# One attention and feed-forward kernel on one core: token chunks taken from one batch, and the second weight matrix kept on the chip for the first unit

## The chip, the core and the metric

The kernel runs on one core of a Trainium2 chip. A core has TensorE (matrix products; its weight loads are a row of their own, PEld, in the profile), VectorE (DVE), ScalarE (ACT), GpSimd (POOL) and SyncE (SP), which here issues most of the DMA transfers. TensorE writes its results to PSUM, from which VectorE and ScalarE read them. Each engine works through its own instructions in the order in which the program issued them, and waits where an operand is not ready. The metric is the time of one execution on the device in microseconds (us); lower is better. The time before is 1080.71 us, the median of three runs.

## What is computed

An attention block without softmax, normed per head, feeds a feed-forward block with a squared ReLU:

```
q, k, v: (8, 8, 576, 64)   # batch, head, position, width of a head; fp32
kv  = einsum('bhsd,bhse->bhde', k, v)          # one 64x64 matrix per batch and head
o   = einsum('bhsd,bhde->bhse', q, kv)
x   = o / sqrt(mean(o*o, -1) + 1e-6) * g_norm  # then (batch*position, head*width) = (4608, 512)
h   = x @ w_in                                 # w_in (512, 2048)
g   = s * max(h, 0)**2 + b
out = g @ w_out                                # w_out (2048, 512)
```

Both weight matrices come to the kernel in a 64-bit type, so that each has to be brought to fp32 on the chip.

## The kernel before

**Tokens.** There are 36 chunks of 128 tokens, numbered c, and 9 units u of four chunks. A chunk takes 64 tokens from each of two batches (a pair is called a group g; positions p*9 + j for one j), so the first chunk needs the k and v of two batches. `load_kv` (L89) brings half of the heads of a group, `load_q` (L102) the q of two chunks.

**kv and attention.** `kv_product` (L271) forms the 64x64 matrices in 64-row, 64-column matmuls and copies them (L292) into `bd_kv`, block diagonal by pairs of heads, with one such block set for each of the two batches. `attention` (L296) has three steps for each chunk: `turn` transposes q (L305, copied at L307), `product` multiplies by `bd_kv` (L317) in two half products per pair of heads, one for each batch, then squares (L326, ACT), sums (L328, DVE), takes the root (L330, ACT) and its reciprocal (L332) and scales (L334, DVE); `turn_x` transposes the result (L342) and copies it to `xT` (L345). `x_sums` (L351) forms four further operands.

**The two large products.** Each is done by a 2x2 block scheme with seven products in place of eight (named x1, z2, x6, y7, x5, x3, y4), whose operands are sums and differences of the blocks and whose results are built up in PSUM banks x, y and z. `mm1` (L386) runs it for each of four strips s of w_in: `keep` (L394) copies a partial result r1, r2 or r4 out of bank x before the next product adds to that bank, VectorE adds it to bank z or y (L164), and `relu_sq` (L383) squares the positive part. The results `ga` stay on the chip. `mm2` (L454) does the same with w_out, for two halves j of a unit; `s2` and `s4` are four VectorE instructions each, on `ga`. It reads the operands of w_out from a ring of three buffers, filled by `load_w2` (L446, issued at L448), one 1 MB transfer per product. The attention of the next unit and `x_sums` run between the steps of mm2 (`side_of`, L607). In every unit x3 and y4 of the last strip come after the first step of mm2.

**The weights.** `load_w` (L119) brings one of sixteen blocks (eight of w_in, eight of w_out, L128 and L133) into one of three raw buffers. `round_w` (L139) converts it: two instructions on ScalarE (L155, L156), then two on VectorE (L158 after L155, L161 after L156). `sum_w_in` (L177) makes further operands of a strip of w_in. `make_w_out` (L203) converts two blocks of w_out, forms the operands for mm2, and stores all seven operand sets to DRAM in pieces (L216 to L223), and `finish_w_out` (L227) adds the blocks to `bias_row` (L259), the row sums times b on TensorE, and makes and stores the last set. All of w_out thus goes to DRAM and comes back for every unit.

**The order.** It is written out by hand. First come the loads and `kv_product` of group 0, the attention of chunks 0 to 3 and the conversion of the first blocks; then mm1 of unit 0, with conversions put between its steps by a table (`in_first`, L641); then the rest of w_out, the loads of q, of the next group's k and v and of the first two w_out operands (all on SP); then mm2 of unit 0. The later units repeat mm1 and mm2; the kv products of groups 1, 2 and 3 are spread over the steps of mm1 in three of them.

Of the kernel before, what the change touches and what calls it, by code (L numbers as in the profile page):

```python
# [15 lines left out]
def kernel(  # L16
# [32 lines left out]

    nc = tc.nc  # L50
# [20 lines left out]
    xp = ctx.enter_context(tc.tile_pool(name="xp", bufs=2))  # L71
    rp = ctx.enter_context(tc.tile_pool(name="rp", bufs=2))
# [14 lines left out]
    HH = H // 2  # L87

    def load_kv(g, half, pool, queues=(nc.sync, nc.sync)):  # L89

        for name, src, queue in zip("kv", (k, v), queues):
            t = pool.tile([P, HH, R, D], FP32, name=f"{name}_sb", tag=name)
            for s in range(2):
                queue.dma_start(
                    out=t[s * HB : s * HB + HB].rearrange("p h j d -> p h (j d)"),
                    in_=src[2 * g + s, half * HH : half * HH + HH].rearrange(
                        "h (p j) d -> p h (j d)", j=R
                    ),
                )
            kv_in[name, g, half] = t  # L100

    def load_q(c, queue=nc.sync):  # L102

        t = qp.tile([P, 2, H, D], FP32, name="q_sb", tag="q")
        for i in range(2):
            g, j = divmod(c + i, R)
            for s in range(2):
                queue.dma_start(  # L108
                    out=t[s * HB : s * HB + HB, i],
                    in_=q[2 * g + s].rearrange("h (p j) d -> p j h d", j=R)[:, j],  # L110
                )
            q_in[c + i] = t[:, i]
# [6 lines left out]
    def load_w(i):  # L119

        dst = convp.tile([P, 2 * words * DM], U32 if wide else FP32, name="w_raw", tag="raw", bufs=3)
# [77 lines left out]
    W2_AT = {1: 0, 7: 1, 5: 2, 6: 3, 4: 4, 2: 5, 3: 6}  # L199
    w2_dram = dram.tile([P, 7, FC // 2, HN], FP32, name="w2")  # L200
    w_up, w_dn = {}, {}

    def make_w_out(s):  # L203

        up = w_up[s] = convp.tile([P, 2, DM], FP32, name="w_up", tag="up", bufs=2)
        dn = w_dn[s] = convp.tile([P, 2, DM], FP32, name="w_dn", tag="dn", bufs=2)
        t = convp.tile([P, 3, 2, HN], FP32, name="w_t", tag="wt", bufs=2)
        b11, b12 = up[:, :, :HN], up[:, :, HN:]
        b21, b22 = dn[:, :, :HN], dn[:, :, HN:]
        t1, t2, t4 = (t[:, i] for i in range(3))  # L210
        blocks = slice(2 * s, 2 * s + 2)

        round_w(FC + 2 * s, up.rearrange("p b n -> p (b n)"))
        sub(t1, b12, b11)
        send_w()
        nc.sync.dma_start(out=w2_dram[:, 0, blocks], in_=b11)  # L216
        round_w(FC + FC // 2 + 2 * s, dn.rearrange("p b n -> p (b n)"))
        sub(t2, b22, t1)
        sub(t4, b21, t2)
        send_w()  # L220
        nc.sync.dma_start(out=w2_dram[:, 2:5, blocks], in_=t)
        for half in range(2):
            nc.sync.dma_start(  # L223
                out=w2_dram[:, 5 + half, blocks], in_=dn[:, :, half * HN : half * HN + HN]
            )

    def finish_w_out(s):  # L227

        bias_row(w_up[s], s == 0, False)
        bias_row(w_dn[s], False, s == NS - 1)  # L230
        b12, b22 = w_up[s][:, :, HN:], w_dn[s][:, :, HN:]
        sub(b12, b22, b12)
        nc.sync.dma_start(out=w2_dram[:, 1, 2 * s : 2 * s + 2], in_=b12)
# [6 lines left out]
    bd_kv = [const.tile([P, 2, NP, P], FP32, name=f"bd_kv_{i}") for i in range(2)]  # L240
# [18 lines left out]
    def bias_row(w, first, last):  # L259

        if first:
            b_ps.append(ps_t.tile([P, DM], FP32, name="b_ps", tag="t"))
        for b in range(2):
            matmul(b_ps[0], b_sq, w[:, b], first and b == 0, last and b == 1)
        if last:
            nc.scalar.copy(b_row, b_ps[0])


    kv_ps = {}

    def kv_product(g, p):  # L271

        if p == 0:
            kv_ps[g] = [ps_t.tile([P, NP, D], FP32, name="kv_ps", tag="t") for _ in range(2)]
        half, h0 = divmod(2 * p, HH)
        kt, vt = kv_in["k", g, half], kv_in["v", g, half]
        for j in range(R):
            for l in range(2):
                for s in range(2):
                    rows = slice(s * HB, s * HB + HB)  # L280
                    nc.tensor.matmul(  # L281
                        kv_ps[g][s][l * HB : l * HB + HB, p, :],
                        lhsT=kt[rows, h0 + l, j, :],
                        rhs=vt[rows, h0 + l, j, :],
                        start=(j == 0),
                        stop=(j == R - 1),
                    )
        if p == NP - 1:
            for s in range(2):
                for l in range(2):  # L290
                    ls = slice(l * HB, l * HB + HB)
                    nc.scalar.copy(bd_kv[g % 2][ls, s, :, ls], kv_ps[g][s][ls])  # L292
# [3 lines left out]
    def attention(c, first=False):  # L296


        bd = bd_kv[c // R % 2]
# [9 lines left out]
        def product():  # L309
# [4 lines left out]
            for p in range(NP):  # L314
                for s in range(2):
                    half = slice(s * HB, s * HB + HB)
                    nc.tensor.matmul(  # L317
                        ps[half, p, :],
                        lhsT=st["qT"][:, p, half],
                        rhs=bd[:, s, p, :],  # L320
                        start=True,
                        stop=True,
                    )
            x = ps.rearrange("p c (l d) -> p (c l) d", l=2)
            sq = attp.tile([P, H, D], FP32, name="sq", tag="sq", bufs=1)
            nc.scalar.activation(sq, x, AF.Square)  # L326
            ss = attp.tile([P, H], FP32, name="ss", tag="ss")
            nc.vector.reduce_sum(ss, sq, axis=mybir.AxisListType.X)  # L328
# [4 lines left out]
            st["xn"] = attp.tile([P, H, D], FP32, name="xn", tag="xn")  # L333
# [4 lines left out]
        def turn_x():  # L338
# [4 lines left out]
            if j == 0:  # L343
                xT[u] = xp.tile([P, KC, 2 * TB], FP32, name="xT", tag="xT", bufs=1)
# [6 lines left out]
    def x_sums(u):  # L351
        b11, b12 = xT[u][:, :KH, :TB], xT[u][:, :KH, TB:]
        b21, b22 = xT[u][:, KH:, :TB], xT[u][:, KH:, TB:]
        for i in (5, 7, 6, 4):
            xs[u, i] = xp.tile([P, KH, TB], FP32, name=f"xs_{i}", tag=f"xs_{i}", bufs=1)
# [27 lines left out]
    def relu_sq(t):  # L383
        nc.vector.scalar_tensor_tensor(t, t, 0.0, t, ALU.max, ALU.mult)  # L384

    def mm1(u, s):  # L386
# [7 lines left out]
        def keep(name, src):  # L394
            st[name] = rp.tile([P, 2, TB], FP32, name=name, tag=name)
            nc.scalar.copy(st[name], src)  # L396

        def x1():
            st["x"] = bank_of("x", "x")
            mm1_product(1, u, s, st["x"], True)  # L400
            keep("r1", st["x"])

        def z2():
# [4 lines left out]
            relu_sq(t)  # L408

        def x6():  # L410
            mm1_product(6, u, s, st["x"], False)
            keep("r2", st["x"])
# [5 lines left out]
        def x5():  # L418
            mm1_product(5, u, s, st["x"], False)
            keep("r4", st["x"])  # L420
            t = g_tile("a22")
            add(t, st["y"], st["r4"])
            relu_sq(t)

        def x3():
# [4 lines left out]
            add(g_tile("s1"), t, ga["a22", s])  # L430
            sub(t, ga["a11", s], t)

        def y4():
# [3 lines left out]
            relu_sq(t)  # L437
# [8 lines left out]
    def load_w2(u, n):  # L446
        t = late["ring"].tile([P, FC // 2, HN], FP32, name="w2_sb", tag="w2")
        nc.sync.dma_start(out=t, in_=w2_dram[:, W2_AT[ORDER[n]]])  # L448
        ring[u, ORDER[n]] = t

    out_v = out.rearrange("(bp j) n -> bp j n", j=R)
    G_OF = {1: "a11", 2: "a12", 3: "a12", 4: "a22", 5: "s1", 6: "a11", 7: "a21"}

    def mm2(u):  # L454
        st = {}

        def product(i, j, ps, first):
            for f in range(FC // 2):
                s, b = divmod(f, 2)
                matmul(  # L460
                    ps, ga[G_OF[i], s][:, b, j * P : j * P + P], ring[u, i][:, f, :],
# [255 lines left out]
```

## Time and profile before

| | |
|---|---|
| Runs | 1077.69, 1080.71, 1099.49 us |
| The profiled execution | 1076.64 us, its span (first to last instruction) 1074.8 us |
| TensorE busy | 999.6 us, 93% of the span |
| VectorE busy | 451.2 us, 42% |
| ScalarE busy | 202.8 us, 19% |
| Moved by DMA | 128.84 MB, 120 GB/s over the span |

The page cuts the span into 40 slices of 26.9 us and gives the busy share of each engine in tenths (9 is 90% or more), and the clock that TensorE was granted, in tenths:

```profile
PE   1788609999999999999999999999999999999998
DVE  0398704244423442444235424443354244524441
ACT  0544400211121112111211121112111211121100
PEclk9889859999999999999999999999999999999999
```

In a timeline row stand the start in us, the length in us, the engine, the line, the operation, what it writes and reads with shapes, and the number of instructions merged; in brackets, how long the engine was idle before and what ended that. In a grouped row the time after the bar is the busy time of the group in us and the mean of one instruction in ns, then the idle time before. A row of transfers has the number, the size of one and the median us from issue to landing.

### The profile page before, as it was taken

To read this page: it belongs to the slowest core of one execution; us is meant where nothing else is said; L and a number is where in the kernel's file an instruction comes from. 1 tells how busy PE (TensorE), PEld (TensorE's weight loads), DVE (VectorE), ACT (ScalarE), POOL (GpSimd) and SP (SyncE) were. 2 spreads that over 40 slices of the span, in tenths; PEclk is the share of its full clock that TensorE was granted. 3 is DMA by queue.
4 is the path that set the end of the run, shared out by engine and by line. 5 is a ranking of instruction groups with operands and counts; after the bars stand their busy time and mean duration, and the time that the engine had idled before them with its cause. 6 is when DMAs were issued, how large, how long until landed. Compare 5 with 4: busy or idle time off the path is not lost.

```text
span 1074.8 us, 13966 instructions
## 1 busy us (share of the span) xinstructions
PE 999.6 (93%) x6080; PEld 857.4 (80%) x6080; DVE 451.2 (42%) x733; ACT 202.8 (19%) x338; POOL 2.5 (0%) x8
## 2 busy tenths in 40 slices
PE   1788609999999999999999999999999999999998
PEld 1577208888888888888888888888888888888887
DVE  0398704244423442444235424443354244524441
ACT  0544400211121112111211121112111211121100
POOL 0000000000000000000000000000000000000000
PEclk9889859999999999999999999999999999999999
DMA  9556792245227222452273224522602260224032
GB/s 196 176 196 215 285 269 101 88 148 128 79 79 210 75 79 88 148 128 79 79 206 79 79 88 147 129 79 79 196 1 79 82 194 1 79 88 147 1 118 79
DMA packets 73838, 128.84 MB, mean 120 GB/s; under 512 B 41136, under 2 KB 45232, under 8 KB 65712
## 3 DMA queue, kind: packets, MB, share of 16 engines
q1 hardware_dynamic: 70128, 125.06, 37.9%
q10 hardware_dynamic: 3648, 2.89, 1.3%
q8 instruction: 48, 0.79, 0.3%
q14 instruction: 14, 0.11, 0.0%
HBM read 111.15 MB, written 16.78 MB: 119 GB/s over the span
## 4 chain that ended last, share of the span: by engine, by line
PE 86%; DMA 5%; DVE 5%; ACT 2%; SPq 1%; issue 1%; ACTq 0%; DVEq 0%
PE x_ps L82 45%; PE y_ps L82 25%; PE z_ps L82 8%; PE x_ps L317 3%; PE kv_ps L281 2%; DMA v_sb<-in_v_dram 2%; PE qT_ps L305 1%; PE xT_ps L342 1%; DMA w_sb<-w 1%; DMA w_raw<-in_moe_w_out_dram 1%; DMA s_col<-in_moe_s_dram 1%; ACT w_raw L156 1%; DMA w_raw<-in_moe_w_in_dram 1%; SPq L108 0%; ACT w_raw L155 0%
## 5 line engine op out<-in xcount | busy, mean ns | idle before, releaser
L82 PE MATMUL x_ps<-w_sb,a 128*128 128x256 f32 x864 | 197.5, 384 | 24.2 <-DMA w_sb<-w 24.2
L82 PEld LDWEIGHTS x_ps<-w_sb,a 128*128 128x128 f32 x864 | 163.6, 192 | 50.1 <-issue 28.5
L82 PE MATMUL y_ps<-w_sb,a 128*128 128x256 f32 x720 | 162.0, 380 | 0.0
L82 PEld LDWEIGHTS y_ps<-w_sb,a 128*128 128x128 f32 x720 | 134.3, 190 | 18.3 <-issue 1.4
L82 PE MATMUL x_ps<-xs,ws 128*128 128x256 f32 x576 | 138.2, 383 | 6.0 <-DVE ws L167 6.0
L82 PE MATMUL y_ps<-xs,wb 128*128 128x256 f32 x576 | 137.7, 382 | 3.4 <-DVE a L164 3.4
L396 ACT COPY r<-x_ps 128x512 f32<-128x512 f32 x108 | 63.3, 586 | 350.9 <-PE x_ps L82 350.9
L82 PEld LDWEIGHTS x_ps<-xs,ws 128*128 128x128 f32 x576 | 110.2, 192 | 21.7 <-issue 6.4
L82 PEld LDWEIGHTS y_ps<-xs,wb 128*128 128x128 f32 x576 | 110.1, 192 | 19.1 <-DVE a L164 3.8
L164 DVE TENSOR_TENSOR a<-y_ps,r 128x512 f32<-128x512 f32 x72 | 49.5, 688 | 138.0 <-ACT r L396 138.0
L466 DVE SCALAR_TENSOR_TENSOR or<-x_ps,s_col,b_row 128x256 f32<-128x256 f32 x54 | 26.1, 483 | 125.2 <-PE x_ps L82 125.2
L384 DVE SCALAR_TENSOR_TENSOR a<-a 128x512 f32<-128x512 f32 x108 | 74.7, 692 | 3.7
L82 PE MATMUL x_ps<-xT,wa 128*128 128x256 f32 x288 | 70.2, 388 | 1.7 <-DVE wa L161 1.7
L82 PE MATMUL x_ps<-xT,ws 128*128 128x256 f32 x288 | 68.5, 380 | 0.2 <-ACT r L396 0.2
L82 PE MATMUL z_ps<-xT,wa 128*128 128x256 f32 x288 | 68.3, 380 | 0.0
L328 DVE TENSOR_REDUCE ss<-sq 128x8 f32<-128x512 f32 x36 | 24.7, 685 | 103.4 <-ACT sq L326 103.3
L82 PE MATMUL x_ps<-w_sb,s 128*128 128x256 f32 x288 | 65.8, 382 | 0.0
L82 PEld LDWEIGHTS x_ps<-xT,wa 128*128 128x128 f32 x288 | 55.5, 194 | 9.9 <-DVE wa L161 2.1
L82 PEld LDWEIGHTS z_ps<-xT,wa 128*128 128x128 f32 x288 | 55.0, 191 | 7.6
L82 PEld LDWEIGHTS x_ps<-xT,ws 128*128 128x128 f32 x288 | 54.4, 190 | 8.0 <-ACT r L396 0.6
L82 PEld LDWEIGHTS x_ps<-w_sb,s 128*128 128x128 f32 x288 | 53.4, 190 | 8.0 <-issue 1.4
L429 DVE TENSOR_TENSOR a<-a 128x512 f32<-128x512 f32 x36 | 24.9, 692 | 73.9 <-ACT a L428 73.9
(64 smaller groups left out, 692.0 us busy)
## 6 DMA issues: line engine op xcount, KB each, us to landing
w_sb<-w SPq DMA_DIRECT2D x63, 1024.0 KB, 5.0
k_sb<-in_k_dram SPq DMA_DIRECT2D x16, 576.0 KB, 7.6
out_dram<-o SPq DMA_DIRECT2D x36, 256.0 KB, 2.1
q_sb<-in_q_dram SPq DMA_DIRECT2D x68, 128.0 KB, 4.5
w_raw<-in_moe_w_in_dram SPq DMA_DIRECT2D x8, 1024.0 KB, 6.4
w_raw<-in_moe_w_out_dram SPq DMA_DIRECT2D x8, 1024.0 KB, 5.8
v_sb<-in_v_dram SPq DMA_DIRECT2D x12, 576.0 KB, 11.5
w<-w_t SPq DMA_DIRECT2D x4, 768.0 KB, 6.8
```

Of the source, the lines that this page charges most:

```text
L82: nc.tensor.matmul(o, lhsT=lhsT, rhs=rhs, start=start, stop=stop, skip_group_check=True)
L156: nc.scalar.activation(lo, lo, AF.Copy, scale=2.0**-29)
L164: nc.vector.tensor_tensor(out=o, in0=a, in1=b, op=ALU.add)
L281: nc.tensor.matmul(kv_ps[g][s][l * HB : l * HB + HB, p, :], lhsT=kt[rows, h0 + l, j, :], rhs=vt[rows, h0 + l, j, :], start=(j == 0), stop= ...
L305: nc.tensor.transpose(ps[:, p, :], q_in[c][:, 2 * p : 2 * p + 2, :], ident)
L317: nc.tensor.matmul(ps[half, p, :], lhsT=st["qT"][:, p, half], rhs=bd[:, s, p, :], start=True, stop=True,)
L328: nc.vector.reduce_sum(ss, sq, axis=mybir.AxisListType.X)
L342: nc.tensor.transpose(ps[:, p, :], st["xn"][:, 2 * p : 2 * p + 2, :], ident)
L384: nc.vector.scalar_tensor_tensor(t, t, 0.0, t, ALU.max, ALU.mult)
L396: nc.scalar.copy(st[name], src)
L429: nc.vector.tensor_mul(t, t, t)
L466: nc.vector.scalar_tensor_tensor(o, ps, s_col, other, ALU.mult, ALU.add)
```

## The change

A chunk is now 128 tokens of one batch: positions j = i and j = 4 + i for i = 0 to 3, and a fifth chunk per pair of batches that takes j = 8 of both (`halves`). k, v, the kv products and `bd_kv` go by batch: `kv_product` runs for one batch in one piece, batch 0 in the head, batch 1 after the third step of mm2 of unit 0, batches 2 to 7 after slot 12 of mm1 of units 1 to 6. `product` does one full matmul per pair of heads where the chunk has one batch. Output rows leave in two transfers per chunk.

For unit 0, w_out's blocks stay on the chip in `w_up` and `w_dn`. Every one of the fourteen conversions after the first two stands at a slot of mm1 (one after it), `bias_row` follows, and the operand sets are formed in place during mm2, each after the product that used the old contents and after the store of them; every set is stored once for the later units. Unit 0 has no ring loads. In unit 0 the squares of z2 and y4 move to ScalarE, the sums s1 and a21 of `ga` are put off to the end of mm1 (`g_sums`), and x3 and y4 of the last strip come before mm2. Several pools go to one buffer, r1 and r4 share one, and the square of the attention output shares a buffer with the scaled output. The first two ring loads of a unit are issued at the end of the unit before.

```diff
+    def halves(c):
+        g, i = divmod(c, R)
+        if i == 4:
+            return [(2 * g, R - 1), (2 * g + 1, R - 1)]
+        b, i = (2 * g, i) if i < 4 else (2 * g + 1, i - 5)
+        return [(b, i), (b, 4 + i)]
...
+    w_up = convp.tile([P, FC // 2, DM], FP32, name="w_up")
+    w_dn = convp.tile([P, FC // 2, DM], FP32, name="w_dn")
+    W2_AT = {
+        1: w_up[:, :, :HN], 6: w_up[:, :, :HN], 5: w_up[:, :, :HN], 7: w_up[:, :, HN:],
+        2: w_dn[:, :, :HN], 4: w_dn[:, :, :HN], 3: w_dn[:, :, HN:],
+    }
+    def sum_w_out(i, fn, a, b):
+        for s in range(NS):
+            blocks = slice(2 * s, 2 * s + 2)
+            fn(W2_AT[i][:, blocks], W2_AT[a][:, blocks], W2_AT[b][:, blocks])
+    def store_w2(*which):
+        for i in which:
+            nc.sync.dma_start(out=w2_dram[i], in_=W2_AT[i])
...
             for p in range(NP):
+                if b == b1:
+                    matmul(ps[:, p, :], st["qT"][:, p, :], bd_kv[b % 2][:, p, :], True, True)
+                    continue
                 for s in range(2):
...
-    def relu_sq(t):
-        nc.vector.scalar_tensor_tensor(t, t, 0.0, t, ALU.max, ALU.mult)
+    def relu_sq(t, on_act):
+        if on_act:
+            nc.scalar.activation(t, t, AF.Relu)
+            nc.scalar.activation(t, t, AF.Square)
+        else:
+            nc.vector.scalar_tensor_tensor(t, t, 0.0, t, ALU.max, ALU.mult)
+    def g_sums(s):
+        add(ga["s1", s], ga["a21", s], ga["a22", s])
+        sub(ga["a21", s], ga["a11", s], ga["a21", s])
...
+        def t2():
+            if u == 0:
+                sum_w_out(6, add, 7, 1)
+                store_w2(6)
+        def t4():
+            if u == 0:
+                sum_w_out(4, sub, 2, 6)
+                store_w2(4)
+        def t1():
+            if u == 0:
+                sum_w_out(5, sub, 3, 6)
+                store_w2(5)
         return [
             lambda: x1(0),
-            seq(lambda: x1(1), nxt(2), s2),
+            seq(lambda: x1(1), nxt(2), t2, s2),
             lambda: z2(0),
-            seq(lambda: z2(1), nxt(3), s4),
+            seq(lambda: z2(1), nxt(3), s4, t4),
             lambda: x6(0),
-            seq(lambda: x6(1), nxt(4)),
+            seq(lambda: x6(1), nxt(4), t1),
...
+    def convert(n):
+        s, lower = divmod(n % FC, 2)
+        if n < FC // 2:
+            round_w_in(s, lower)
+            send_w()
+            if lower:
+                sum_w_in(s)
+        else:
+            round_w_out(s - NS, lower)
+            send_w()
...
-    in_first = {0: (convert_w_in, 1), 4: (convert_w_in, 2), 11: (convert_w_in, 3), 17: (make_w_out, 0)}
+    at_slot = {0: 2, 2: 3, 4: 4, 7: 5, 9: 6, 12: 7, 15: 8, 18: 9, 20: 10, 22: 11, 24: 12, 26: 13, 27: 14}
...
         if u == 0:
-            finish_w_out(0)
-            for s in range(1, NS):
-                make_w_out(s)
-                finish_w_out(s)
-            tc_late()
+            convert(15)
+            for i in range(2):
+                load_kv(1, i, convp, tag="raw", bufs=3)
             loads(0)
-            load_w2(0, 0)
-            load_w2(0, 1)
+            bias_row()
+            store_w2(1, 2, 3)
+            sum_w_out(7, sub, 3, 7)
+            store_w2(7)
+            for s in range(NS):
+                g_sums(s)
```

More of the change, by code (lines that the diff above doesn't have):

```diff
@@ L257 @@
     b_ps = []
[L259 to L277, printed above, removed]
-            for l in range(2):
[L279 to L292, printed above, removed]
@@ new lines, in bias_row, with kv_product @@
+    def bias_row():
+        ps = ps_t.tile([P, DM], FP32, name="b_ps", tag="t")
+        blocks = [w[:, 2 * s + b] for s in range(NS) for w in (w_up, w_dn) for b in range(2)]
+        for n, w in enumerate(blocks):
+            matmul(ps, b_sq, w, n == 0, n == FC - 1)
+        nc.scalar.copy(b_row, ps)
+    def kv_product(b):
+        ps = [ps_t.tile([P, 2, D], FP32, name="kv_ps", tag="t") for _ in range(2)]
+        for i in range(2):
+            kv = kv_in.pop((b, i))
+            for j in range(R):
+                for l in range(2):
+                    for r in range(2):
+                        rows = slice(r * HB, r * HB + HB)
+                        nc.tensor.matmul(
+                            ps[r][l * HB : l * HB + HB, i, :],
+                            lhsT=kv[rows, 0, l, j, :],
+                            rhs=kv[rows, 1, l, j, :],
+                            start=(j == 0),
+                            stop=(j == R - 1),
+                        )
+        for r in range(2):
+            for l in range(2):
+                ls = slice(l * HB, l * HB + HB)
+                nc.scalar.copy(bd_kv[b % 2][ls, 2 * r : 2 * r + 2, ls], ps[r][ls])
@@ L580 @@
         send_w()
-    for p in range(NP):
-        kv_product(0, p)
+    kv_product(0)
     kv0p.release()
```

191 lines of the change are left out of this document (85 added, 106 removed).

## The prediction

> **What bounds the kernel now.** I read the busy time by stage first, then the timeline of the head and of the first unit, then one late unit on TensorE, and the chain of waits at the one long hole. In the stage rows the columns are window, length, busy PE, PEld, DVE, ACT, POOL, granted clock, DMA share, GB/s.
>
> ```profile
> span 1074.8 us, 13966 instructions
> 0.00:46.70 46.70, 18.11 (x384) 15.07 (x384) 8.73 (x17) 12.50 (x23) 2.48 (x8) 0.90 0.80 192
> 46.70:106.80 60.10, 50.50 (x208) 42.72 (x209) 50.37 (x70) 26.37 (x32) 0.00 (x0) 0.91 0.59 201
> 106.80:159.20 52.40, 19.35 (x34) 6.68 (x32) 21.18 (x27) 14.05 (x14) 0.00 (x0) 0.68 0.88 268
> 171.88:1029.43 857.55, 857.55 (x5217) 745.93 (x5217) 355.96 (x592) 149.27 (x268) 0.00 (x0) 1.00 0.34 101
> 819.26:924.35 105.09, 105.09 (x546) 91.67 (x545) 44.50 (x74) 18.11 (x32) 0.00 (x0) 1.00 0.28 91
> 603.47:714.18 110.71, 110.71 (x833) 95.89 (x833) 44.48 (x74) 19.57 (x36) 0.00 (x0) 1.00 0.37 108
> 145.01 13.77 DMA w_sb<-w
> 159.23 5.74 PE L82 MATMUL x_ps<-w_sb,a 128*128 128x256 f32 x16 [24.23 <-DMA w_sb<-w]
> ```
>
> From 171.88 us, where z2 of the first unit's mm2 starts, TensorE has no gap, at full clock: a unit takes 105.09 us, 110.71 with a pair of batches' kv products, so a wait there must become a gap before it costs, and only fewer TensorE cycles gain. Before it, 172 us hold one unit's worth of TensorE work: the head waits for k and v, the first mm1 runs beside VectorE (50 of 60 us busy), and from 106.8 to 159.2 TensorE does 19 us of work while w_out is converted, sent to DRAM and read back. That is what the change touches.
>
> **The head.** Before, two batches' k and v land; afterwards one batch's.
>
> ```profile
> 16.22 4.03 PE L281 MATMUL kv_ps<-v_sb,k_sb 64*64 64x64 f32 x142 [3.27 <-DMA v_sb<-in_v_dram]
> 27.18 3.71 PE L281 MATMUL kv_ps<-v_sb,k_sb 64*64 64x64 f32 x142 [5.11 <-DMA v_sb<-in_v_dram]
> 30.97 1.51 ACT L292 COPY bd_kv<-kv_ps 64x256 f32<-64x256 f32 x4 [28.96 <-PE kv_ps L281]
> 45.30 0.67 ACT L345 ACTIVATE xT<-xT_ps,g_col 128x512 f32<-128x512 f32 x1
> 46.70 3.78 PE L82 MATMUL x_ps<-xT,wa 128*128 128x256 f32 x8 [1.67 <-DVE wa L161]
> ```
>
> The first half-load, whose bytes equal one batch's, was complete at 16.2. I keep 16.2: transfers are half as large, but q moves up beside them. Then the second pair of heads' products, half of 3.71 (1.9), and four copies of half the width, 0.26 each by estimate from 0.38: 19.2 against 32.5. From there to the fourth xT (45.97) are 13.5 us of unchanged attention. Call that end E: 45.97 before, 32.7 afterwards. w_raw follows q with 10 us to spare.
>
> **The first mm1.** Afterwards it carries all sixteen conversions, on in-order queues.
>
> ```profile
> L155 ACT ACTIVATE w_raw<-w_raw 128x1024 f32<-128x1024 f32 x16 | 18.6, 1160 | 9.2 <-DMA w_raw<-in_moe_w_out_dram 9.2
> L156 ACT ACTIVATE w_raw<-w_raw 128x1024 uint32<-128x1024 uint32 x16 | 18.5, 1157 | 0.0
> L158 DVE TENSOR_SCALAR w_dn<-w_raw 128x1024 uint32<-128x1024 uint32 x4 | 2.8, 689 | 0.4 <-ACT w_raw L155 0.4
> L161 DVE CUSTOM_DVE_ANT_0 w_dn<-w_raw,w_dn 128x2048 uint16<-128x2048 uint16 x4 | 4.9, 1225 | 0.8 <-ACT w_raw L156 0.3
> L167 DVE TENSOR_TENSOR ws<-ws,wa 128x512 f32<-128x512 f32 x4 | 2.8, 692 | 0.1
> L164 DVE TENSOR_TENSOR a<-y_ps,r 128x512 f32<-128x512 f32 x72 | 49.5, 688 | 138.0 <-ACT r L396 138.0
> L396 ACT COPY r<-x_ps 128x512 f32<-128x512 f32 x108 | 63.3, 586 | 350.9 <-PE x_ps L82 350.9
> L428 ACT ACTIVATE a<-x_ps 128x512 f32<-128x512 f32 x36 | 21.5, 598 | 100.1 <-PE x_ps L82 100.1
> 106.99 1.88 PE L82 MATMUL b_ps<-w_up,b_sq 128*128 128x512 f32 x4
> 108.71 1.88 PE L82 MATMUL b_ps<-w_dn,b_sq 128*128 128x512 f32 x4
> w_raw<-in_moe_w_out_dram SPq DMA_DIRECT2D x8, 1024.0 KB, 5.8
> w<-w_t SPq DMA_DIRECT2D x4, 768.0 KB, 6.8
> ```
>
> A conversion is 2.2 us on ACT (two instructions overlapping a little), then 1.25 on DVE for its last step; sum_w_in 2.6 (four overlapping L167 of 0.69); an add 0.7; Relu then Square, now on ACT for z2 and y4 of unit 0, 1.2; a keep copy 0.6; a warm mm1 product 1.73, a cold one up to 3.8 (the 46.70 row). The move to ACT makes a ring: the Square waits for DVE's add, the add stands behind a conversion on DVE, that waits for ACT, and the next keep, which lets TensorE write the x bank again, stands behind all of it. I follow the start of x5 in each strip, in us after E. Strip 0: conv0's last step and cold x1 to 4.55, keep 0.6, conv1 2.1 on ACT, 1.2 on DVE, two sums 1.5, so x6 at 10.0; conv2's end and z2's add on DVE to 13.75, 1.2, keep to 15.5, y7 ending at 16.4: x5 at 16.4. Strip 1: conv3 behind that keep (2.1, 1.25) and its sum_w_in 2.6 end at 21.4; then x5's add and relu 1.4, conv4 2.0, x3's multiply and z2's add 1.3, ACT 1.2, conv5 2.2 and 1.2, sums 2.6, y4's add 0.6, ACT 1.2, keep 0.6: 35.7. Strip 2: cold x5 3.8, x1 2.9, keep 0.6, conv7 2.1 and 1.3, sums 2.6, three DVE steps 1.9, ACT 2.4 less 0.7 that overlaps, conv8 2.1, keep 0.5: 55.2. Strip 3 the same way without sums, conv9 to conv11: 16.3, so 71.5. To the end: x5 2.3, keep 0.6, x3 1.9, Relu 0.6, conv13 2.2 and 1.2, add 0.7, ACT 1.2, conv14 and conv15 4.3, last DVE step 1.3: 87.8. Each block's load goes out at least 9 us before its turn, against 5.8 to land.
>
> Bias_row, 32 instructions of 0.43 (four in 1.72, the two b_ps rows), is 13.8 us, free before in a hole; now it starts after y4 at 77.9, waits for the last blocks, and ends at 91.7. So its cover is mostly the last conversions; without them it would cost all 13.8. mm2 starts at E + 91.7, its z2 6.9 later: 32.7 + 98.6 = 131.3 against 171.88 before, which is 40.6 us less. The DRAM round trip is the largest part of it.
>
> **mm2 of the first unit.** Operands are made in place, so DVE now waits for stores: t2 for store 1, t1 for store 6. SP issues eight kv transfers from E + 80 (they wait for converted raw tiles), eight q, then the stores at E + 93. With 2.36 MB of kv, 1.05 of q and 1.05 of store at the first stage's 192 to 268 GB/s, store 1 lands at about E + 103, t2 and s2 are done at 108.5, and x6 wants them at 109.8 (91.7, four products of 3.45, kv 2.8, attention 1.5). Later stores each follow 4.5 us on; store 6 at E + 121 holds DVE, and behind it the norm of chunk 5, whose turn is due at 126. I put 2 us of stall, bounds 0 and 17 (rival B). Queued behind on SP are only out stores and loads for unit 1, 50 us early.
>
> **Later units.** kv: 7 batches at half of 5.62 (110.71 less 105.09) are 19.7 against 16.9, plus 2.8. Attention of one batch: 8 full instructions for 16 half ones.
>
> ```profile
> 822.55 0.60 PE L305 MATMUL qT_ps<-ident,q_sb 128*128 128x128 f32 x4
> 822.99 3.62 PE L82 MATMUL y_ps<-w_sb,a 128*128 128x256 f32 x16
> 826.54 1.09 PE L317 MATMUL x_ps<-bd_kv,qT 128*64 128x128 f32 x16
> 827.56 3.72 PE L82 MATMUL x_ps<-w_sb,a 128*128 128x256 f32 x16
> 831.12 0.60 PE L305 MATMUL qT_ps<-ident,q_sb 128*128 128x128 f32 x4
> w_sb<-w SPq DMA_DIRECT2D x63, 1024.0 KB, 5.0
> out_dram<-o SPq DMA_DIRECT2D x36, 256.0 KB, 2.1
> ```
>
> Start to start, 16 halves take 1.02 and the next product 0.1 more than its 3.45. Full 128-column instructions go at 0.11 each (0.44 for four): 8 are 0.88. The saving is 0.14 to 0.35 a chunk; over the 28 later chunks of one batch (36 less 4 in the head and 4 mixed) 4 to 9.8 us. I take 0.25, or 7, between them as the 0.1 may stay. The Trainium skill, "TensorE: Matmul & The Clock Gate", Part 3 on packing small matmuls, says that tiles in different column groups run at once for about 4 ns more a tile; by that a pair of halves would already cost what one full product does, nearly nothing would be saved, and the time would be about 1041 (rival E). The trace here has 0.128 a pair, above 0.11, so it bears the rule out in part only.
>
> Single buffers for r, x and xs: in the strip, the copy into "ra" waits for the add of the strip before; by the rows it is 0.4 us early, and TensorE needs the copy only three products later. Nothing. Square into xn, kv in one block, shared tags: the readers are two slots earlier; nothing. Output stores double in number; the last pair adds one issue, 0.6 at the end.
>
> **Sum.** 131.3, plus 902.9 (1074.8 less 171.88), plus 2.8, less 7, plus 2, plus 0.6: span 1032.6. The profiled execution took 1076.64 for its span of 1074.8, so 1034.4; it stands 4.1 under the median of the runs (1080.71) and 1.1 under the lowest. I say 1035.
>
> **Rivals.**
> A, the ring of waits does not bite: unit 0 falls to its loads, TensorE 0.7 + 3.8 + 27 × 1.73 + 13.8 = E + 65, DVE E + 57: 27 us less, 1008. For it: VectorE was 84% busy in that stage; against: the queues are in order.
> B, stores follow one another at 9.1 us each (768 KB in 6.8): store 6 lands at E + 142, t1 at 145, x5 of mm2 wants it at 127.5: 17 more, 1052. For it: the w_t row; against: 268 GB/s with many transfers at once.
> C, the head is no earlier, since q's small rows and w_raw share the transfers: 13 more, 1047. Against: the 16.2 above.
> D, slower: w2 loads come late. y7's load goes out two products (with attention 8.9 us) ahead; landing takes 5.0. Above 8.9 every one of five loads in eight units makes a gap; from 10.6 us on, 40 × 1.7 = 68, the kernel is 2% slower, about 1103. Against: DMA share 0.28 there, with the same bytes.
> E, the halves were as quick as full products, no saving of 7: 1042. Against: 1.02 against 0.88.
>
> **How the numbers follow.** Forecast 0.52 with its own range 1020 to 1046 (E by 3, the strips by 6, attention by 3, stalls by 5); A 0.12, B 0.15, C 0.07, D 0.04, E 0.10. Leaving out A and D, 0.16, the range is 1016 to 1052. Faster than 1059 (2%, about what a measurement tells from no change): all but D and a few of B and C's tails: 0.93; within 0.04; slower 0.03.
>
> **What would show it.** kv products start at 16 and x1 at 33; bias at E + 78 to 92, with no w_sb before mm2 of unit 0; DVE idle before L161 and ACT idle before the Squares in the strips, TensorE waiting for r ahead of x5; t2 and t1 waiting for stores or not; units of about 104 us, 107 with kv. An idle gap in a late unit, or x1 at 45, would prove me wrong.

## The result and the profile after

The changed kernel takes 1032.4 us, the median of four runs (1030.88 to 1034.46), against 1079.2 for the kernel before in its four: a ratio of 0.958, with a 95% interval of 0.954 to 0.961. The ratio leaves out the one run of the kernel before, 1099.49 us, that lies 2% above its others. The forecast was 1035 with a range of 1016 to 1052. The profiled execution took 1031.52 us, with a span of 1029.7.

From the page of the kernel after, the span, TensorE's busy share in 40 slices of 25.7 us, and the costliest group in which TensorE waits (busy, mean ns, then the idle time before it and what ended most of that):

```profile
span 1029.7 us, 13548 instructions
PE   4668899999999999999999999999999999999998
L84 PE MATMUL x_ps<-xs,ws 128*128 128x256 f32 x576 | 142.6, 392 | 18.7 <-ACT r L396 14.8
```

The hole between 107 and 159 us is gone. What is left of TensorE's idle time lies mostly in the first five slices. Its largest piece there is the last row: x5 and x6 of mm1 wait 18.7 us, and 14.8 of them end with a copy of r on ScalarE. The chain of waits gives the start of z2 of unit 0's mm2, the mark of the forecast:

```profile
134.32 3.45 PE z_ps L84 x16
```

That is 37.6 us earlier than the 171.88 of before. In the busy time by stage (start and end, length, busy PE, PEld, DVE, ACT, POOL, granted clock, DMA share, GB/s), the first rows are the head, the first mm1 and bias_row; then stand a unit with a kv product, one without, and the tail:

```profile
0.00:35.04 35.04, 15.76 (x208) 14.02 (x209) 8.81 (x18) 12.16 (x23) 1.63 (x8) 0.99 0.72 188
35.04:113.31 78.27, 58.92 (x224) 48.22 (x225) 47.77 (x63) 42.75 (x55) 0.00 (x0) 0.85 0.52 174
113.31:127.04 13.73, 13.73 (x34) 6.27 (x33) 9.39 (x13) 6.88 (x8) 0.00 (x0) 1.00 0.72 162
244.08:350.32 106.24, 106.24 (x658) 93.93 (x657) 44.46 (x74) 19.15 (x36) 0.00 (x0) 1.00 0.38 112
880.02:983.80 103.78, 103.78 (x513) 91.81 (x513) 44.47 (x74) 18.11 (x32) 0.00 (x0) 1.00 0.24 81
983.80:1029.70 45.90, 41.44 (x192) 36.13 (x191) 11.09 (x21) 0.00 (x0) 0.00 (x0) 0.98 0.36 115
```

The first mm1 takes 78.27 us, and no engine explains it by its share: TensorE is busy for 58.92, VectorE for 47.77 (61%), ScalarE for 42.75 (55%). From 134.32 on, up to the tail, TensorE is idle for 0.67 us in all, so only fewer TensorE cycles count there, and the units are shorter than the 105.09 of before.

The timeline shows the ring of waits of the forecast in strip 1:

```profile
62.24 0.69 DVE L165 TENSOR_SCALAR wb<-w_raw 128x1024 uint32<-128x1024 uint32 x1 [2.36 <-ACT w_raw L162]
67.06 0.68 DVE L171 TENSOR_TENSOR a<-y_ps,r 128x512 f32<-128x512 f32 x1
67.77 0.63 ACT L377 ACTIVATE a<-a 128x512 f32<-128x512 f32 x1 [4.55 <-DVE a L171]
68.43 0.63 ACT L378 ACTIVATE a<-a 128x512 f32<-128x512 f32 x1
68.97 0.57 ACT L396 COPY r<-x_ps 128x512 f32<-128x512 f32 x1
69.59 3.78 PE L84 MATMUL x_ps<-xs,ws 128*128 128x256 f32 x8 [7.83 <-ACT r L396]
89.04 3.68 PE L84 MATMUL x_ps<-xs,ws 128*128 128x256 f32 x8 [4.23 <-ACT r L396]
```

Read it from the last wait backwards. TensorE stood for 7.83 us at x5 for a copy of 0.57. What it copies was complete when x6 ended at 60.04 (58.15 and 1.89), but the copy stood on ScalarE behind Relu and Square (L377, L378), and its only buffer still held the r2 that y4's add was to read. Relu and Square waited 4.55 us for that add on VectorE, which stood there behind a conversion and the sums of a strip. And that conversion had waited 2.36 us for ScalarE. After the wait, eight instructions whose row shows 1.89 where TensorE had no wait take 3.78.

The head, and then the way from the last conversion through bias_row to store 1 (the transfer of operand set 1 to DRAM) and to the sums that overwrite set 1, t2 at 137.19 and t1 at 153.85, in the timeline:

```profile
20.42 2.05 PE L84 MATMUL x_ps<-bd_kv,qT 128*128 128x128 f32 x8
33.63 0.67 ACT L337 ACTIVATE xT<-xT_ps,g_col 128x512 f32<-128x512 f32 x1
35.04 3.38 PE L84 MATMUL x_ps<-xT,wa 128*128 128x256 f32 x8 [2.12 <-DVE wa L168]
113.52 1.88 PE L84 MATMUL b_ps<-w_up,b_sq 128*128 128x512 f32 x4
122.14 1.23 DVE L168 CUSTOM_DVE_ANT_0 w_dn<-w_raw,w_dn 128x2048 uint16<-128x2048 uint16 x1 [0.29 <-ACT w_raw L163]
127.26 7.07 PE L84 MATMUL x_ps<-w_up,a 128*128 128x256 f32 x32
137.19 2.50 DVE L171 TENSOR_TENSOR w_up<-w_up 128x512 f32<-128x512 f32 x4 [2.34 <-DMA w<-w_up]
145.80 3.72 PE L84 MATMUL x_ps<-w_up,a 128*128 128x256 f32 x16
153.85 2.48 DVE L174 TENSOR_TENSOR w_up<-w_dn,w_up 128x512 f32<-128x512 f32 x4
```

VectorE does wait for store 1 (2.34 us ahead of t2), but x6 at 145.80 has no wait.

### The profile page after: what moved, and what is told of

It is laid out like the page before. It is cut to its first block, busy times and chain, and to the rows that moved or that the text cites. A ratio compares the mean times of both kernels' runs of the same rounds, so it can differ in the third digit from the quotient of the medians.

```text
span 1029.7 us, 13548 instructions
## 1 busy us (share of the span) xinstructions
PE 985.9 (96%) x5824; PEld 860.0 (84%) x5824; DVE 444.9 (43%) x725; ACT 214.4 (21%) x370; POOL 1.6 (0%) x8
## 4 chain that ended last, share of the span: by engine, by line
PE 91%; ACT 3%; DVE 2%; DMA 2%; issue 0%; DVEq 0%
PE x_ps L84 51%; PE y_ps L84 26%; PE z_ps L84 8%; PE qT_ps L295 2%; PE kv_ps L272 2%; PE xT_ps L334 1%; PE b_ps L84 1%; ACT w_raw L163 1%; ACT w_raw L162 1%; DMA kv_sb<-in_v_dram 1%; DMA q_sb<-in_q_dram 1%; DVE wb L168 0%; DMA w_raw<-in_moe_w_in_dram 0%; ACT a L378 0%; ACT a L377 0%
## 5 line engine op out<-in xcount | busy, mean ns | idle before, releaser
L84 PE MATMUL x_ps<-w_sb,a 128*128 128x256 f32 x768 | 172.3, 379 | 0.0
L84 PE MATMUL x_ps<-xs,ws 128*128 128x256 f32 x576 | 142.6, 392 | 18.7 <-ACT r L396 14.8
L84 PEld LDWEIGHTS x_ps<-w_sb,a 128*128 128x128 f32 x768 | 144.3, 190 | 18.9 <-issue 0.2
L84 PE MATMUL y_ps<-w_sb,a 128*128 128x256 f32 x640 | 143.4, 379 | 0.0
L84 PEld LDWEIGHTS x_ps<-xs,ws 128*128 128x128 f32 x576 | 112.6, 196 | 36.6 <-ACT r L396 16.5
L84 PEld LDWEIGHTS y_ps<-w_sb,a 128*128 128x128 f32 x640 | 119.4, 190 | 15.2 <-issue 0.2
L380 DVE SCALAR_TENSOR_TENSOR a<-a 128x512 f32<-128x512 f32 x100 | 69.2, 692 | 3.4
L468 DVE SCALAR_TENSOR_TENSOR or<-x_ps,s_col,b_row 128x256 f32<-128x256 f32 x54 | 26.0, 482 | 89.1 <-PE x_ps L84 89.1
L321 DVE TENSOR_REDUCE ss<-xn 128x8 f32<-128x512 f32 x36 | 24.6, 684 | 85.4 <-ACT xn L319 85.3
L84 PEld LDWEIGHTS z_ps<-xT,wa 128*128 128x128 f32 x288 | 54.7, 190 | 7.4
L84 PE MATMUL x_ps<-w_sb,s 128*128 128x256 f32 x256 | 57.8, 380 | 0.0
L84 PEld LDWEIGHTS x_ps<-w_sb,s 128*128 128x128 f32 x256 | 47.6, 190 | 6.1 <-issue 0.2
```

The costliest lines, as they stand in the source:

```text
L84: nc.tensor.matmul(o, lhsT=lhsT, rhs=rhs, start=start, stop=stop, skip_group_check=True)
L321: nc.vector.reduce_sum(ss, st["xn"], axis=mybir.AxisListType.X)
L468: nc.vector.scalar_tensor_tensor(o, ps, s_col, other, ALU.mult, ALU.add)
```

## The experiments

The theory: a ring in the first mm1, made by the squares' move to ScalarE; w_out's round trip through DRAM gone; one batch's k and v ahead of the head; and full products in place of half ones. Spans are compared with 1029.7. Each is that of one profiled execution, and the runs of one kernel differ by 1.6 to 6 us. In the profiled executions whose head is unchanged mm1 starts between 33.9 and 35.8 us (in one at 39.6, after a wait of 4.08 us for q). So 1 or 2 us of a span show little alone.

**The ring: the squares back on VectorE, and a second buffer for r2.** For unit 0's z2 and y4, and for the r2 of odd strips:

```diff
-            relu_sq(t, u == 0)
+            relu_sq(t, False)
...
         def keep(name, src, tag):
-            st[name] = rp.tile([P, 2, TB], FP32, name=name, tag=tag)
+            if tag == "rb" and u == 0 and s % 2:
+                st[name] = outp.tile([P, DM], FP32, name="o1", tag="o1").rearrange("p (b n) -> p b n", b=2)
+            else:
+                st[name] = rp.tile([P, 2, TB], FP32, name=name, tag=tag)
```

> The changed kernel with the squares of z2 and y4 of unit 0 back on VectorE (8 instructions of 0.69 us more there, 16 of 0.63 less on ScalarE), and a second buffer for r2 of the odd strips of unit 0, so that ScalarE no longer waits for VectorE's adds ahead of a keep. Theory (a ring of waits between ScalarE and VectorE paces the first mm1, not the load of either): TensorE's idle time ahead of x5 of the strips (7.8, 4.2 and 2.7 us) shrinks by half or more, and mm2 starts 5 to 12 us earlier, with a gain of the span of 4 to 10. Rival (the move of the squares is a gain, as VectorE's load is what paces the stage): 8 x 0.69 = 5.5 us slower.

Measured: 1012.77 us, ratio to the kernel before 0.939 (0.937 to 0.941); the span is 1009.8, 19.9 less. The mechanism held, and the size expected was too small. The stage row and the same group of x5 and x6:

```profile
34.69:93.38 58.69, 51.77 (x224) 43.36 (x225) 51.58 (x70) 35.22 (x42) 0.00 (x0) 0.97 0.63 214
```

```profile
L84 PE MATMUL x_ps<-xs,ws 128*128 128x256 f32 x576 | 136.4, 379 | 5.4 <-DVE ws L174 3.7
```

With 3.8 us more work on VectorE the first mm1 is 19.6 us shorter. The group accounts for nearly all of it: 13.3 us less waiting (18.7 to 5.4), and 6.2 less busy time (142.6 to 136.4), since TensorE hardly runs slowly after a wait any more (the granted clock of the stage is 0.97, where it was 0.85). Two further runs split the two edits.

**Only the squares back on VectorE.**

> The changed kernel with only the squares of z2 and y4 of unit 0 back on VectorE, r2 in one buffer as the change has it. The pair with the second buffer fell by 20 us. Theory one (the ring closes in two places, the Square ahead of the keep on ScalarE, and the one r2 buffer, whose reader is VectorE's add; with the squares gone the keep still waits for that add): the gain is 3 to 9 us, well short of 20. Theory two (the squares on ScalarE alone made the ring): 17 to 20 us.

Measured: 1017.83 us, 0.942 (0.940 to 0.945), span 1014.9, 14.8 less. The result lies between the two expectations.

```profile
L84 PE MATMUL x_ps<-xs,ws 128*128 128x256 f32 x576 | 138.5, 384 | 8.3 <-ACT r L396 4.5
```

Again the group accounts for it: 10.4 less waiting and 4.1 less busy. The squares' place is thus about three quarters of the 19.9.

**Only the second buffer.**

> The changed kernel with only the second buffer for r2 of the odd strips of unit 0, the squares on ScalarE. Theory one and theory two alike: the Square stands ahead of the keep on ScalarE's queue and waits for the same add, so no change within 2 us. Rival (the buffer alone was the limit): 10 us or more faster.

Measured, in a single run: 1031.47 us, span 1029.7, no change.

```profile
69.77 1.65 PE L84 MATMUL x_ps<-xs,ws 128*128 128x256 f32 x3 [7.81 <-ACT o L399]
```

The wait at x5 is 7.81 where it was 7.83: the copy has a free buffer and still stands behind the Square. The buffer gains only where the squares are gone: the spans with and without it are then 5.1 apart. The group accounts for that too (2.9 less waiting, 2.1 less busy), but the intervals of the two ratios overlap, so the size is rough.

**ScalarE's part of a conversion, one conversion earlier.** VectorE's part then finds its operand ready. `act_part` issues the two ScalarE instructions of a conversion.

```diff
+        if n > 0:
+            for m in (n, n + 1):
+                if m < len(blocks) and blocks[m] in w_raw:
+                    act_part(blocks[m], w_raw[blocks[m]])
```

> The changed kernel with the two ScalarE instructions of each conversion after the first issued one conversion ahead of the two on VectorE. Theory (VectorE's waits of 2.4 to 2.9 us for ScalarE ahead of each conversion are links of the ring that paces the first mm1): some 2.3 us less for each of the five or six conversions on that chain, mm2 starts about 10 us earlier, the span falls by 7 to 12. Rival (the waits are slack, TensorE's work or the keep copies set the pace): no change within 2 us.

Measured: 1022.53 us, 0.948 (0.946 to 0.951), span 1019.4, 10.3 less, as the theory had it.

```profile
L84 PE MATMUL x_ps<-xs,ws 128*128 128x256 f32 x576 | 141.0, 389 | 10.1 <-ACT r L406 7.2
```

The wait falls by 8.6 and the busy time by 1.6. So the ring can be cut at another of its links.

**All three cuts together.**

> The squares of unit 0 on VectorE, the second buffer for r2, and ScalarE's part of each conversion one conversion ahead. Alone, the first two gained 20 us and the third 10. Theory (they break the same ring): together they gain 0 to 4 us over the 20, since TensorE then runs almost without a gap from 66 us on. Rival (they remove different waits): 8 to 10 us over the 20, 1003 us.

Measured: 1012.86 us, 0.938 (0.935 to 0.940), span 1011.2. As the theory had it, that is no more than the first experiment gave (1012.77): the edits remove the same waits.

**The round trip: the first operand of unit 0 read back from DRAM.** One of the seven sets is stored and read again before it is used.

```diff
-            w2 = W2_AT[i] if u == 0 else ring[u, i]
+            w2 = ring[u, i] if u > 0 or i == 1 else W2_AT[i]
...
             store_w2(1, 2, 3)
...
+            nc.sync.dma_start(out=back, in_=w2_dram[1])
+            ring[0, 1] = back
```

> The changed kernel with the first of the seven w_out operands of unit 0 stored to DRAM and read back before x1 of mm2, as the kernel before did with all seven; the other six stay on the chip. Theory (the round trip stands on the path between the last conversion and mm2): the read goes out when store 1 has landed (137 us in the changed kernel) and takes 5 to 10 us behind two more stores, so x1 of mm2 starts at 142 to 147 instead of 127 and the span grows by 14 to 19 us. Rival (bias_row and the conversions cover it): less than 4 us.

Measured: 1055.42 us, 0.977 (0.973 to 0.980), span 1049.9, 20.2 more.

```profile
145.75 8.72 PE L84 MATMUL x_ps<-w_back,a 128*128 128x256 f32 x32 [19.11 <-DMA w_back<-w]
```

x1 starts 18.5 us later than in the kernel after (127.26), and takes 8.72 in place of 7.07 after the wait: together 20.1. The slow products after the wait bring it a little above the 14 to 19 that were expected. One store and one load on the path, with the transfers queued ahead of them, thus cost more than half of the 37.6 us by which z2 comes earlier.

**The head: batch 1's k, v and kv product ahead of the first chunk too**, and not in mm2.

```diff
-    kv0p = tc.alloc_tile_pool(name="kv0p", bufs=2)
+    kv0p = tc.alloc_tile_pool(name="kv0p", bufs=4)
     for i in range(2):
         load_kv(0, i, kv0p, (nc.sync, nc.scalar), tag="kv")
+    for i in range(2):
+        load_kv(1, i, kv0p, (nc.sync, nc.scalar), tag="kv")
...
     kv_product(0)
+    kv_product(1)
...
-        if u == 0:
-            side[2].insert(0, lambda: kv_product(1))
...
-            for i in range(2):
-                load_kv(1, i, convp, tag="raw", bufs=3)
```

> The changed kernel with k, v and the kv product of batch 1 in the head again, beside batch 0, instead of in mm2 of unit 0. Theory (the head waits for its bytes): x1 of mm1 starts at 45 to 47 us instead of 35.0, mm2 of unit 0 is 3.1 shorter, the span grows by 7 to 10 us. Rival (w_raw, q and the attention chain set the head): x1 within 3 us of 35, and the span the same or a little shorter.

Measured: 1040.32 us, 0.964 (0.961 to 0.966), span 1036.3, 6.6 more.

```profile
45.85 1.65 PE L84 MATMUL x_ps<-xT,wa 128*128 128x256 f32 x3 [1.91 <-DVE wa L168]
```

mm1 starts 10.8 us later, close to the 46.70 of before, about 3 us come back in mm2, where the kv product is gone, and about 1 in mm1, where x5 of strip 3 takes 1.99 us instead of 3.48 after the same wait. The half load in the head is worth about 11 us of the 37.6. With the 20 of the round trip that is most of it, if the two add up, which no run tests.

**Attention by half products.** Every chunk does sixteen half products again, both halves with the one batch's matrix.

```diff
-                if b == b1:
-                    matmul(ps[:, p, :], st["qT"][:, p, :], bd_kv[b % 2][:, p, :], True, True)
-                    continue
...
-                        rhs=bd_kv[(b + s) % 2][:, p, :],
+                        rhs=bd_kv[(b1 if s else b) % 2][:, p, :],
```

> The changed kernel with the attention product done in two half products per pair of heads for every chunk, as before the change. Theory (a half pair costs more than a full product in the row of 128-column instructions): the interval from z2 to z2 of a unit without kv products goes from 103.78 back to 105.1 us, 1.30 more for four chunks, and over the 28 later chunks of one batch the span grows by 9.1 us (28 x 0.325); the head, where ScalarE and VectorE set the pace, hardly changes (within 1 us). Rival (halves in different column groups run at the same time and cost no more than a full product): the interval stays at 103.8 to 104.0 and the span within 1.5 us.

Measured: 1041.05 us, 0.965 (0.962 to 0.968), span 1040.2, 10.5 more (the medians are 8.7 apart). Of the 10.5, 1.1 is a later start of mm1, in a head where TensorE waits 2.54 us for q, so that this part need not come from the halves. The unit without a kv product and one chunk of it:

```profile
784.06:889.15 105.09, 105.09 (x546) 91.65 (x545) 44.50 (x74) 18.12 (x32) 0.00 (x0) 1.00 0.28 91
791.34 1.09 PE L307 MATMUL x_ps<-bd_kv,qT 128*64 128x128 f32 x16
792.36 3.72 PE L84 MATMUL x_ps<-w_sb,a 128*128 128x256 f32 x16
```

And the same place in the kernel after:

```profile
779.64 3.62 PE L84 MATMUL y_ps<-w_sb,a 128*128 128x256 f32 x16
783.10 1.05 PE L84 MATMUL x_ps<-bd_kv,qT 128*128 128x128 f32 x8
783.99 3.62 PE L84 MATMUL x_ps<-w_sb,a 128*128 128x256 f32 x16
787.44 0.60 PE L295 MATMUL qT_ps<-ident,q_sb 128*128 128x128 f32 x4
```

The unit is 105.09 again, as before the change, against 103.78. Start to start, the attention product went from 1.02 to 0.89, and both its neighbours got shorter: the product after it from 3.56 to 3.45, and the one ahead of it from 3.55 to 3.46 (by the rows of before). That is 0.33 a chunk, the 1.31 of a unit over four chunks. Two halves side by side therefore cost more than one full product. The Trainium skill, "TensorE: Matmul & The Clock Gate", Part 3 on packing small matmuls, gives about 4 ns for each further tile; here a pair of halves costs 16 ns more than a full product in its own slot (0.13 us over eight pairs), and 41 with its neighbours (0.33), so for these fp32 products the measurement decides.

**The bias: from one of its sixteen blocks.** The other fifteen are left out of the bias.

```diff
         for n, w in enumerate(blocks):
-            matmul(ps, b_sq, w, n == 0, n == FC - 1)
+            if n == 0:
+                matmul(ps, b_sq, w, True, True)
```

> The changed kernel with bias_row made from one block of w_out in place of sixteen: 2 instructions for 32, 12.9 us less TensorE work between y4 of the last strip and mm2. The output lacks the bias of the fifteen other blocks. Theory (the bias stands on the path, but the last conversions and the store of the first operand set are late next): x1 of mm2 starts at once but can't end before the conversion at 121.3 us, z2 of mm2 starts at about 125.5 instead of 133.95, then x6 waits for t2 and s2, which wait for store 1 at about 137: the span falls by 3 to 6 us, not by 12.9. Rival (nothing else is late there): 12.9 us less. Second rival (the conversions cover the bias): no change within 1 us.

Measured: 1027.92 us, 0.953 (0.951 to 0.956), span 1025.9, 3.8 less.

```profile
105.34 1.99 PE L84 MATMUL x_ps<-xs,ws 128*128 128x256 f32 x8 [2.74 <-ACT r L397]
119.24 6.27 PE L84 MATMUL x_ps<-w_up,a 128*128 128x256 f32 x20 [4.06 <-DVE w_up L168]
136.65 2.50 DVE L171 TENSOR_TENSOR w_up<-w_up 128x512 f32<-128x512 f32 x4 [6.89 <-DMA w<-w_up]
139.80 5.41 PE L84 MATMUL x_ps<-w_up,a 128*128 128x256 f32 x16 [2.75 <-DVE a L174]
```

The bias took 13.7 us of TensorE, and 12.9 of them are gone, but the span falls by only 3.8 (the medians by 4.5), and mm1 started 1.15 us earlier here (33.89). So the bias is worth some 3 to 4.5 us, as the theory had it. The last conversions are next: mm2 stands 4.06 us for a block of w_out. Then come the stores: t2 now waits 6.89 us for store 1, and x6 stands 2.75 for what is queued behind t2.

**The same, with store 1 ahead of q on SP's queue.**

```diff
+            store_w2(1)
             loads(0)
             bias_row()
-            store_w2(1, 2, 3)
+            store_w2(2, 3)
```

> The run with the bias from one block of w_out (the output lacks the bias of the other fifteen), and store 1 issued ahead of the eight q transfers instead of behind them. In that run VectorE waited 6.89 us for store 1 ahead of t2, and x6 of mm2 started 2.75 us late. Theory (with the bias gone, store 1 is late next): t2 starts at least 5 us sooner, x6 has no wait, and the span falls by 2 to 4 us more. Rival (x6 waits for VectorE's own queue, not for the store): within 1 us.

Measured: 1025.63 us, 0.949 (0.948 to 0.951), span 1023.1, 2.8 less than the run before it (the medians are 2.3 apart, and the intervals of the two ratios just meet).

```profile
104.93 3.68 PE L84 MATMUL x_ps<-xs,ws 128*128 128x256 f32 x8 [2.74 <-ACT r L397]
131.51 2.50 DVE L171 TENSOR_TENSOR w_up<-w_up 128x512 f32<-128x512 f32 x4 [0.48 <-DMA w<-w_up]
139.01 3.72 PE L84 MATMUL x_ps<-w_up,a 128*128 128x256 f32 x16
```

t2 runs 5.1 us sooner and x6 no longer waits. So the store's place in the queue was the second cover of the bias.

**A bias that costs TensorE little.** The first experiment, store 1 ahead of q, and the blocks of w_out summed on GpSimd as they are converted, so that TensorE needs two instructions for the bias.

```diff
+        for b in range(2):
+            nc.gpsimd.tensor_tensor(out=b_acc[0], in0=b_acc[0], in1=w[:, 2 * s + b], op=ALU.add)
...
-        for n, w in enumerate(blocks):
-            matmul(ps, b_sq, w, n == 0, n == FC - 1)
+        matmul(ps, b_sq, b_acc[0], True, True)
```

> The squares on VectorE and the second buffer for r2, with the sixteen blocks of w_out added up on GpSimd as they are converted, so that the bias takes 2 TensorE instructions instead of 32, placed after x1 of mm2, and with store 1 ahead of q. All of the computation is kept. Theory (with the ring gone TensorE bounds the first unit, and the bias is 13.8 us of its work): 12.9 us less on TensorE, of which the last conversions and the stores give some back: 7 to 12 us below the 1012.8 of the run with the first two. Rival (GpSimd's adds are slow, or slow VectorE's instructions beside them): the adds end after 115 us or VectorE's 0.69 us instructions grow, and the time is 1012 or more.

Measured: 1020.74 us, 0.945 (0.942 to 0.947), some 8 us slower than the first experiment (1012.77) and than the three cuts (1012.86, on the same chip), neither of which has any of it. The theory failed, and the rival held.

```profile
85.58 1.77 DVE L165 TENSOR_SCALAR w_up<-w_raw 128x1024 uint32<-128x1024 uint32 x1
95.33 3.81 POOL L261 TENSOR_TENSOR o<-o,w_dn 128x512 f32<-128x512 f32 x2 [2.66 <-DVE w_dn L168]
95.93 2.09 DVE L168 CUSTOM_DVE_ANT_0 w_up<-w_raw,w_up 128x2048 uint16<-128x2048 uint16 x1
104.34 0.68 DVE L171 TENSOR_TENSOR a<-y_ps,o 128x512 f32<-128x512 f32 x1
112.16 5.68 DVE L174 TENSOR_TENSOR w_up<-w_dn,w_up 128x512 f32<-128x512 f32 x4
116.74 2.07 PE L84 MATMUL b_ps<-o,b_sq 128*128 128x512 f32 x2 [5.19 <-POOL o L261]
```

While GpSimd adds, a conversion's last step on VectorE takes 2.09 in place of 1.23, and four differences of 2.5 take 5.68. The conversions end at 112.2 us, where they end at 100.9 in the first experiment, and TensorE waits for them. Then it stands 5.19 us for the last sum. The work left the engine that was busy and slowed the one that now sets the pace.

> The version before this one with ScalarE's part of each conversion one conversion ahead. With TensorE's bias gone the conversions pace the end of the first mm1 again. Theory: 1 to 5 us below the version before this one. Rival (ScalarE's keeps wait longer behind two conversions): the same or slower.

With ScalarE's part drawn forward as well: 1017.53 us, 0.943 (0.940 to 0.945), 3.2 less than without that by the medians and within the theory's 1 to 5, but the intervals of the two ratios overlap, so that a gain is not shown. It is 4.7 slower than the three cuts, from which it differs only in the bias and the store.

The best versions are the first experiment (the squares back on VectorE and a second r2 buffer, 1012.77 us) and the three cuts (1012.86), the same within the noise and both faster than the kernel before and the kernel after.

## Why the prediction was right

**The head, right, 1.6 short.** E was put at 32.7 and came at 34.30 (33.63 and 0.67). The copies end at 19.0, as forecast (19.2). The term that failed is "13.5 us of unchanged attention", which took 15.3: the first product takes 2.05 us in this head, and the same product, in sixteen halves, took 1.09 in the head of the kernel before, so TensorE was still slow here.

```profile
33.24 1.09 PE L317 MATMUL x_ps<-bd_kv,qT 128*64 128x128 f32 x16
```

Rival C falls: x1 is at 35.04, and only with two batches ahead is it at 45.85.

**The ring, right.** x5 of strips 1 and 2 was put at E + 35.7 and 55.2, and stands at 35.3 and 54.7 (69.59, 89.04). The last conversion was to end at E + 87.8, and ends at 89.1 (122.14 and 1.23). mm2 was to start at E + 91.7, and starts at 93.0 (127.26). A list of in-order steps, each with a duration from a row, was within 1.3 us over 90. The 1.3 is one term, x5 of strip 3, put at 2.3 us where it took 3.48. That the agreement is this close is in part luck: over the seven kernels that have this ring the first mm1 differs by up to 1.3 us, and that x5 takes 1.99 us in three of them and 3.48 to 3.68 in four. Rival A (no ring, 27 less) does not happen, but it is near what the kernel can have: without the squares on ScalarE and with a second buffer the span is 19.9 less. The forecast named the move as the ring's cause and did not say that undoing it would gain 15 to 20 us.

**bias_row's cover, right.** It was said to be hidden mostly by the last conversions. It costs some 3 to 4.5 us, and the stores are its second cover, which the forecast had not named.

**The stores, the mechanism right, the size wrong.** Store 1 was to land at E + 103, and t2 starts at 137.19, E + 102.9. The 2 us of stall were 0: t2 waits, but what follows it is in time for x6. t1, which follows store 6, starts at 153.85, E + 119.6, without a wait (forecast: store 6 at E + 121). Rival B had it at E + 145 and falls; its own terms, four stores of 9.1 behind E + 103, give 139 for store 6 and not 142.

**Later units, two sizes wrong.** The attention saving was taken as 0.25 a chunk, 7 us; it is 0.33, which over 28 chunks is 9.2, because the 0.1 at the product behind, said to perhaps stay, is gone, and as much goes at the product ahead. Rival E falls with the half products' 105.09. The kv term was taken as half of the 5.62 for a pair; a unit with one batch's product is 106.24 less 103.78, or 2.46, longer. Seven of these are 17.2 against the 16.9 of before, so the term of 2.8 should have been 0.3.

**The sum.** z2 came 3.0 later than forecast (134.32 against 131.3). From there to the end are 895.4 us (1029.7 less 134.3), where the forecast had 901.3 (902.9 plus 2.8, less 7, plus 2, plus 0.6). The errors of +3.0 and -5.9 give the 2.9 by which the span was forecast too long, so it is luck that the total is closer than its parts. The -5.9 is made up, within 0.2, of 2.5 from the kv term, 2.2 from the attention and the 2 of stall, less a gap of 0.67 that the forecast did not have: in mm2 of unit 0 TensorE waits at 140.73 for ScalarE's copies of batch 1's kv product. Rival D shows nowhere: the later units have no gap.

## What to carry to other kernels

Where two engines hand work to each other, write down the queue of each in order and follow one copy through both: an instruction that waits for the other engine costs everything queued behind it, above all a copy that frees a PSUM bank, and the busy shares (61% and 55% here) do not show it. Before taking work off a path, ask what is late next, and price that too: 12.9 us of exposed TensorE work were worth some 3 to 4.5. Work moved to an idle engine is free only if it takes nothing from the engine that sets the pace.

## What the hardware showed unexpectedly

**The price of a wait depends on when it falls.** The rows 105.34 and 104.93 of the two bias kernels are the same x5 after the same wait of 2.74 us; in one the eight instructions take 1.99 us at a granted clock of 1.00, in the other 3.68 at 0.54. Over the seven kernels with the ring, x5 of strip 3 has the same wait of 2.72 to 2.74 and takes 1.99 in three and 3.48 to 3.68 in four. The Trainium skill, "TensorE: Matmul & The Clock Gate", Part 1, says that the clock follows activity in a free-running window of about 3.4 us, and that the moment at which it rises depends on where in the window the first matmul lands; an outcome that changes from one kernel to the next after the same wait fits that. The same Part 1 of the Trainium skill puts the slow state behind at least one idle window; here a wait of about 2.7 us was enough in four of the seven, and the measurement decides. The waits of 4.23 and 7.83 both cost the slow rate (3.68 and 3.78).

**GpSimd slows VectorE, but not all of it.** Beside a GpSimd add, conversions went from 1.23 to 2.09 us and differences from SBUF from 2.5 to 5.68 for four, while the add with an operand in PSUM stayed at 0.68. A conversion's first step on VectorE, with one operand in SBUF, went from 0.69 to 1.77. The Trainium skill, "GPSIMD Engine Reference", section 1, says that GpSimd's SBUF interfaces are shared with VectorE, with contention for VectorE instructions that have two SBUF inputs or run in a 2-port mode. The rows agree for those with two inputs and for the one in PSUM; no row shows in which mode the first step ran.

**A matmul on half of the columns reaches its neighbours.** The products ahead of and behind the half products are each 0.1 us longer; no run shows why.
